# Value rows spaced 72 columns apart in place of 66, in an attention and mixer kernel on one core

## The chip, the core and the metric

The kernel runs on one core of one Trainium2 chip. The metric is the device time of one execution in microseconds; the median of several executions stands for a kernel. The profile is of one such execution.

## The reference

The first half is cosine attention over 8 batches of 12 heads, 448 positions and 64 columns a head. The second half is a low-rank token mixer followed by a two-layer network (768 to 3072 to 768 columns), with residuals.

```python
q_n = q / (norm(q) + 1e-6);  k_n = k / (norm(k) + 1e-6)
scores = q_n @ k_n.T / tau
attn = exp(scores - max(scores));  attn = attn / (sum(attn) + 1e-9)
x = (attn @ v) as [batch, position, 768]
h = x.T @ U @ V                      # rank 32, over positions
u = x + h.T
out = u + relu(u @ w_ch1) @ w_ch2
```

## The kernel before

**Planning.** The kernel does not issue its instructions as it describes them. It adds operations to a planner (`Plan`), each with an engine, an assumed duration, its dependencies and its buffers. The planner simulates the five engines and the order of starts in that simulation becomes the program. TensorE takes its operations from ten streams of fixed priority, and the products below are in one of them (`pe_av`), so that they are put between the long products of the two-layer network (`pe_mlp`). No duration in the plan depends on how the value buffer is laid out.

**Scores and exponents.** For each batch and each pair of heads, `scores` (L677) multiplies keys by queries into PSUM, and ScalarE writes the exponents as bf16 into an `attn` tile (L695, L690), keys on the partitions. There are four key blocks `j`: of 112 keys each in batches 0 and 1, of 128, 128, 128 and 64 in the others, where two neighbouring pairs share one tile for the short block.

**Values.** Two tiles `v_nat` (`v_t`, L327) take turns over the batches. One holds, on each partition, 12 heads by 4 key blocks of rows of D + 2 = 66 bf16 columns: 64 values and two ones. The 65th column makes the product with the exponents also give their sum. The rows are filled by casting DMAs from GpSimd's queue (L516 in batches 0 and 1, L519 and L524 in the others), the ones and the zero halves by memsets on VectorE (`set_v` L1011; `set_v_tiles` L1015, L1017, L1018).

**The product** (`values`, L717 to L721) is a stationary 128-query block of `attn` against one row of 65 columns of `v_nat`. Each head has four query blocks `t`, each a region of 65 columns in one PSUM bank, and each region is summed over the four key blocks:

```python
out=av.tile[:, t, 0:D + 1],
lhsT=(attn if j < SC - 1 else even).tile[0:kp, j, hh, 128 * t:128 * (t + 1)],
rhs=v_t[b % 2][0:kp, h, j, 0:D + 1], start=start, stop=(j == SC - 1),
```

They come in two orders. For all heads but two, `t` is the outer loop and `j` the inner one (L740, L741): four products in a row sum into one region, each from another row of `v_nat`. For the last pair of heads of batch 0 (`ends`, L724 to L731) it is the other way round: for each `j` and head, the four query blocks follow each other, so that four products in a row read the same row of `v_nat` and sum into four different regions. There are 8 x 12 x 16 = 1536 products.

VectorE then takes the reciprocal of the 65th column (L746) and scales the 64 others into `X_sb` (L748). The mixer follows (L801, then L772 and L777 in batch 0, L851 and L865 in the others), then the two-layer network (L928, L951 or L953, L964, L975) and the output DMAs.

Of the kernel before, what the change touches and what calls it, by code (L numbers as in the profile page):

```python
# [12 lines left out]
BF = mybir.dt.bfloat16  # L13
# [256 lines left out]
def kernel(  # L270
# [14 lines left out]
    B, H, S, D = q.shape  # L285
# [7 lines left out]
    SC = 4  # L293
# [18 lines left out]
    def fixed(n, shape, dt, name):  # L312

        tiles = [const.tile(shape, dt, name=f"{name}{i}") for i in range(n)]
        return tiles
# [8 lines left out]
    ld_t = fixed(3, [SCH, 2, G, SC * D], BF, "qk_nat")  # L324
    xn_t = fixed(3, [SCH, 2 * SC, 128], BF, "xn")
    attn_t = fixed(3, [128, SC, 2, 512], BF, "attn")
    v_t = fixed(2, [128, H, SC, D + 2], BF, "v_nat")  # L327

    r_ld, r_xn, r_attn = fixed_ring(ld_t), fixed_ring(xn_t), fixed_ring(attn_t)
    r_sq = ring(2, [SCH, G // 2, SC * D], BF, "sq")  # L330
# [855 lines left out]
```

## Time and profile before

| | |
|---|---|
| median of 9 executions | 585.07 us (584.55 to 586.47) |
| the profiled execution's own time | 585.07 us |
| its span, first to last instruction | 583.3 us |
| mean granted TensorE clock | 0.999 |
| TensorE busy | 573.7 us (98%) |
| VectorE, ScalarE, GpSimd busy | 293.2, 285.0, 93.0 us |
| the 1536 value products (L718): first to last start | 19.1 to 470.7 us |

The profiled execution's time is the median, and 1.8 us of it lie outside the span. A matmul's recorded duration includes its way through the array: consecutive products overlap, so 193 ns is the recorded duration of a value product, while the next one starts some 30 ns after it. What a product costs its engine is the distance from its start to the next start. In a merged row of the timeline, a run of n products lasts n - 1 such distances and one duration.

### The profile page before, as it was taken

Reading aid. Unit: us, or ns where it says so; the run is one execution under the profiler, and the core shown is the slowest. Engines: PE = TensorE matmul, PEld = TensorE weight load, DVE = VectorE, ACT = ScalarE, POOL = GpSimd, SP = SyncE. Lnnn points to the kernel's source line nnn. Section 1 sums busy time; section 2 is a strip of 40 time slices with the busy share of each in tenths; the row PEclk is TensorE's granted clock in tenths of the full one; section 3 lists DMA queues with packets and bytes.
Section 4 is the critical chain, followed back from the end, with each engine's and each line's share of the span. In section 5 each row is a group of like instructions: output and inputs, shape, how many; then the busy total and the mean of one; then the engine's idle time right before and its main releaser. Section 6 shows DMA issues by size and latency. Waiting matters only on the chain.

```text
span 583.3 us, 11692 instructions
## 1 busy us (share of the span) xinstructions
PE 573.7 (98%) x4850; PEld 329.4 (56%) x4871; DVE 293.2 (50%) x690; ACT 285.0 (49%) x471; POOL 93.0 (16%) x134
## 2 busy tenths in 40 slices
PE   8899999999999999999999999999999999999997
PEld 6565656445655665554466655655456666654565
DVE  8979829999656676557434660343102241100011
ACT  7977754677625671466543645434454334024300
POOL 8234240161050132003300140000000000000000
PEclk9999999999999999999999999999999999999999
DMA  9999992997594479346945572231041100310021
GB/s 157 198 207 190 210 159 63 147 130 109 91 124 107 68 80 144 74 78 77 86 88 97 105 49 68 61 74 33 0 67 30 42 15 8 89 40 1 1 54 56
DMA packets 133429, 50.69 MB, mean 87 GB/s; under 512 B 98304, under 2 KB 133376, under 8 KB 133376
## 3 DMA queue, kind: packets, MB, share of 16 engines
q0 software_dynamic: 72256, 25.73, 39.3%
q1 hardware_dynamic: 61056, 24.19, 19.9%
q8 instruction: 38, 0.62, 0.4%
q14 instruction: 15, 0.12, 0.1%
q10 hardware_dynamic: 64, 0.02, 0.0%
HBM read 52.25 MB, written 11.01 MB: 108 GB/s over the span
## 4 chain that ended last, share of the span: by engine, by line
PE 94%; DVE 3%; ACT 1%; issue 1%; DMA 1%; DVEq 0%
PE bank L964 38%; PE bank L928 37%; PE bank L718 8%; PE bank L677 7%; PE bank L851 2%; DVE xn L618 1%; PE bank L474 1%; DVE ss L550 1%; PE bank L801 1%; ACT attn L690 1%; DMA raw_uv<-in_q_dram 1%; ACT sq L544 0%; DVE qkT L1005 0%; PE bank L772 0%; DVE X_sb L748 0%
## 5 line engine op out<-in xcount | busy, mean ns | idle before, releaser
L964 PE MATMUL bank<-w_sb,relu 128*128 128x384 bf16 (+1 forms) x1368 | 231.6, 323 | 0.3 <-DVE X_sb L748 0.2
L928 PE MATMUL bank<-uT,w_sb 128*128 128x384 bf16 (+1 forms) x1132 | 229.8, 352 | 1.2 <-ACT sq L544 0.2
L695 ACT ACTIVATE attn<-bank 128x896 bf16<-128x896 f32 (+1 forms) x166 | 141.1, 916 | 98.5 <-PE bank L677 98.4
L964 PEld LDWEIGHTS <-relu 128*128 128x128 bf16 x1368 | 128.6, 98 | 90.2 <-issue 12.5
L928 PEld LDWEIGHTS <-w_sb 128*128 128x128 bf16 x1152 | 109.1, 98 | 102.3 <-issue 7.6
L951 ACT ACTIVATE relu<-bank 128x384 bf16<-128x384 f32 (+1 forms) x156 | 84.6, 543 | 131.0 <-PE bank L928 130.0
L975 DVE TENSOR_TENSOR O_sb<-bank,u_nat 128x384 f32<-128x384 f32 (+1 forms) x57 | 31.2, 549 | 183.9 <-PE bank L964 162.3
L550 DVE TENSOR_REDUCE ss<-sq 112x8 f32<-112x512 bf16 x96 | 62.4, 673 | 1.9 <-ACT sq L544 1.4
L718 PEld LDWEIGHTS <-attn 128*128 128x128 bf16 (+1 forms) x1536 | 56.0, 98 | 10.0 <-issue 2.8
L618 DVE TENSOR_TENSOR xn<-qk_nat,inv 112x512 bf16<-112x512 bf16 x93 | 60.4, 680 | 0.1
L718 PE MATMUL bank<-v_nat,attn 128*128 128x65 bf16 (+1 forms) x1536 | 59.2, 193 | 0.1
L677 PE MATMUL bank<-qkT 64*128 64x448 bf16 (+1 forms) x384 | 50.1, 358 | 1.5 <-ACT attn L690 0.8
L746 DVE RECIPROCAL rd<-bank 128x4 f32<-128x4 f32 x96 | 16.9, 178 | 59.4 <-PE bank L718 56.6
L496 POOL DMA_DIRECT2D qk_nat<-in_q_dram x24 | 17.3, 723 | 176.6 <-issue 63.3
L748 DVE TENSOR_TENSOR X_sb<-bank,rd 128x256 bf16<-128x256 f32 x96 | 40.2, 421 | 2.0
L544 ACT ACTIVATE sq<-qk_nat 112x512 bf16<-112x512 bf16 x51 | 31.1, 630 | 8.4 <-DVE ss L550 7.9
L519 POOL DMA_DIRECT2D v_nat<-in_v_dram x36 | 26.6, 746 | 49.3 <-PE bank L718 45.4
L953 DVE TENSOR_SCALAR relu<-bank 128x512 bf16<-128x512 f32 (+1 forms) x36 | 22.6, 628 | 14.6 <-PE bank L928 14.4
L677 PEld LDWEIGHTS <-qkT 64*128 64x128 bf16 (+1 forms) x384 | 13.5, 95 | 28.5 <-issue 24.1
L865 DVE TENSOR_TENSOR u_nat<-bank,X_sb 128x384 bf16<-128x384 f32 (+2 forms) x45 | 21.8, 525 | 12.2 <-PE bank L851 12.0
L496 POOL DMA_DIRECT2D qk_nat<-in_k_dram x24 | 16.9, 703 | 4.1 <-DMA w_sb<-in_moe_w_ch_dram 3.6
L546 DVE TENSOR_TENSOR sq<-qk_nat 112x512 bf16<-112x512 bf16 x43 | 16.9, 414 | 0.2
(59 smaller groups left out, 188.5 us busy)
## 6 DMA issues: line engine op xcount, KB each, us to landing
qk_nat<-in_q_dram POOLq DMA_DIRECT2D x23, 224.0 KB, 4.9
qk_nat<-in_k_dram POOLq DMA_DIRECT2D x23, 224.0 KB, 5.7
w_sb<-in_moe_w_ch_dram POOLq DMA_DIRECT2D x4, 1152.0 KB, 21.6
w_sb<-in_moe_w_ch_dram POOLq DMA_DIRECT2D x8, 576.0 KB, 15.9
out_dram<-O_sb SPq DMA_DIRECT2D x15, 168.0 KB, 2.3
v_nat<-in_v_dram POOLq DMA_DIRECT2D x14, 168.0 KB, 9.7
out_dram<-O_sb SPq DMA_DIRECT2D x16, 144.0 KB, 2.1
out_dram<-O_sb SPq DMA_DIRECT2D x16, 120.0 KB, 2.3
```

Of the source, the lines that this page charges most:

```text
L496: ops = [load(lambda i=i, src=src: nc.gpsimd.dma_start(out=ld.tile[:, i, lo:lo + h1 - h0, :], in_=src[b, h0:h1].rearrange("h (s c) d -> s ...
L544: nc.scalar.activation(out=y, in_=x, func=AF.Square)
L550: lambda i=i, a0=a0, a1=a1, sq=sq: nc.vector.reduce_sum(ss.tile[:, i, a0:a1, :].rearrange("p h c -> p (h c)"), sq.tile[:, 0:a1 - a0, :].re ...
L618: nc.vector.tensor_mul(dst, src, sc)
L677: nc.tensor.matmul(out=out, lhsT=qkT.tile.rearrange("p b s -> p (b s)")[r, n0:n0 + w], rhs=qkT.tile[r, SC:2 * SC, :].rearrange("p c s -> p ...
L695: exps.append(plan.add(Op("ACT", act_t(2 * S, 0.08), lambda sc=sc, c=c, attn=attn: nc.scalar.activation(out=attn.tile[0:SCH if b < WIDE el ...
L718: nc.tensor.matmul(out=av.tile[:, t, 0:D + 1], lhsT=(attn if j < SC - 1 else even).tile[0:kp, j, hh, 128 * t:128 * (t + 1)], rhs=v_t[b % 2 ...
L748: muls.append(plan.add(Op("DVE", dve_t(256), lambda av=av, rd=rd, h=h: nc.vector.tensor_mul(X.tile[:, :, h * D:(h + 1) * D], av.tile[:, :, ...
L928: o = plan.add(Op("PE", pe_t(n), lambda cc=cc: nc.tensor.matmul(out=mm.tile[:, 0:n], lhsT=w1_sb[:, cc, f * 128:(f + 1) * 128], rhs=uT.tile ...
L951: nc.scalar.activation(out=relu.tile[:, f, 0:n], in_=mm.tile[:, 0:n], func=AF.Relu)
L964: nc.tensor.matmul(out=mm.tile[:, 0:c1 - c0], lhsT=relu.tile[:, f, i * 128:(i + 1) * 128], rhs=w2_t[:, f, c0:c1], start=(f == 0), stop=(f ...
L975: nc.vector.tensor_add(out=O.tile[:, 0:w], in0=mm.tile[:, 0:w], in1=us[i].tile[:, c0:c1]),
```

## The change

The rows of both value tiles get 72 columns in place of 66. A row is then 144 bytes long in place of 132. The products, the DMAs and the memsets address the same columns as before (64 values and the ones at columns 64 and 65); the columns 66 to 71 are used by nothing, except that the memset of a whole row (L1018) also sets them.

```diff
-    v_t = fixed(2, [128, H, SC, D + 2], BF, "v_nat")
+    v_t = fixed(2, [128, H, SC, D + 8], BF, "v_nat")
```

A tile starts at a multiple of 64 bytes in both kernels. Before, row (h, j) begins 132 (4 h + j) bytes into it, so the four key blocks begin 0, 4, 8 and 12 bytes past a multiple of 16. After, every row begins at a multiple of 16. Each tile grows from 6336 to 6912 bytes on a partition, and every tile that is allocated behind them moves up by 1152 bytes, which is a multiple of 64. The order of instructions is the same on every engine; only the memset at L1018 has another shape, 64 x 216 words in place of 64 x 198.

## Prediction

> **What bounds the kernel now.** I read the page from the top: busy shares and slices, then the chain that ended last.
>
> ```profile
> PE 573.7 (98%) x4850; PEld 329.4 (56%) x4871; DVE 293.2 (50%) x690; ACT 285.0 (49%) x471; POOL 93.0 (16%) x134
> PE   8899999999999999999999999999999999999997
> PEclk9999999999999999999999999999999999999999
> PE 94%; DVE 3%; ACT 1%; issue 1%; DMA 1%; DVEq 0%
> ```
>
> TensorE is busy throughout at full clock and carries 94% of the chain. So a nanosecond taken from each TensorE product comes off the end, and what another engine or a queue does is hidden unless TensorE comes to wait for it. The lines that the change touches, in the groups of instructions and the waits of TensorE after 40 us:
>
> ```profile
> L718 PE MATMUL bank<-v_nat,attn 128*128 128x65 bf16 (+1 forms) x1536 | 59.2, 193 | 0.1
> PE bank L964 <- DVE X_sb L748: 0.2, 1, 0.2
> PE bank L928 <- ACT sq L544: 0.2, 1, 0.2
> ```
>
> The value products waited 0.1 us in all, and after 40 us TensorE waited 0.4 us for other engines. A gain on these products would be kept almost whole.
>
> **What a value product costs now.** I took the start of each of the 1536 records and the distance to the next start where that is a value product too, and sorted the distances by key block j, that is, by how far the row begins past a multiple of 16 bytes. Outside the last head pair of batch 0, leaving out one distance over 60 ns: j = 0 (0 bytes) 29.3 ns on average over 374 distances; j = 1 (4 bytes) 33.2 over 374; j = 2 (8 bytes) 32.5 over 373; j = 3 (12 bytes) 32.6 over 323. For j = 0 the median is 29 for each of the 12 heads.
>
> That looks like the price of a misaligned row: (3.9 + 3.2 + 3.3) ns x 376 query blocks (94 heads by 4) = 3.9 us. But j = 0 differs from the rest in a second way: it opens its PSUM region, and j = 1 to 3 add to the region that the product just before them wrote. The trace holds places where the two come apart. I read these timeline rows:
>
> ```profile
> 34.71 0.78 PE L718 MATMUL bank<-v_nat,attn 112*128 112x65 bf16 x20
> 35.41 0.24 PE L801 MATMUL bank<-X_sb,U_sb 128*32 128x128 bf16 x4
> ...
> 185.34 1.18 PE L718 MATMUL bank<-v_nat,attn 128*128 128x65 bf16 x32
> ```
>
> The row at 185.34 is two heads in the usual order: (1.18 - 0.19) / 31 = 31.8 ns a product, as 8 distances of 29.3 and 23 of about 32.8 would make it. The row at 34.71 belongs to the last head pair of batch 0, where four products in a row read one row of values and go to four different regions. It has 19 distances; the first two, after a wait, are 38 and 36 ns, and the other 17 come to 507 ns, 29.8 each. Of the 20 products 16 read misaligned rows, and 16 add to a region that holds a sum already. At 33 ns a misaligned read, these would take some 33 each; their distances are 30, 29, 32, 29, 30, 29, 32, 29, 30, 29, 33, 29, 29, 30, 29. So neither a misaligned row nor adding as such costs the 3 to 4 ns; adding to the region that was written just before does, or else changing rows does.
>
> The second place:
>
> ```profile
> 58.29 0.35 PE L718 MATMUL bank<-v_nat,attn 112*128 112x65 bf16 x6
> 58.49 0.36 PE L474 MATMUL bank<-ident,xn 112*128 112x112 bf16 x4
> 58.68 0.48 PE L718 MATMUL bank<-v_nat,attn 112*128 112x65 bf16 x10
> ```
>
> Four transposes cut a region's sum in two. The row at 58.68 begins with j = 2, 8 bytes past a multiple of 16, and a row not read just before. Its distance is 29 ns; the next product, j = 3, takes 35, and then j = 0 29 again, j = 1 32. The same cut in batch 1, head 5 lets a j = 1 product start fresh: 29, then 35. A misaligned product on a region that was not written just before costs what an aligned one does. I hold the order of sums to be the cause, and the change does not touch that order.
>
> **The change part by part.** *1128 misaligned products outside the last pair of batch 0* (94 heads x 12): become aligned. Bounds from the rows above: 0 by the two natural tests, -3.9 us by the distances sorted by j. I take 0: the tests change the order and keep the misalignment, the sorting changes both. A loss is excluded by j = 0, whose rows are aligned already and are the quick ones, in heads where they lie at 0 and at 16 past a multiple of 32. *24 in the last pair*: they stand up to 0.8 ns above 29; 0.0 us.
>
> [...]
>
> *Memsets*: four at L1018 grow from 198 to 216 words. One takes 223 ns; 223 x 18/198 = 20 ns at most, 80 ns for all, on VectorE at 38 and 99 us, where the chain runs through TensorE. I take 0; if that cover were gone, +0.08 us.
>
> *Value DMAs*: 43008 packets of 128 bytes, to rows 144 bytes apart in place of 132. Their records last 31 or 32 ns in four of five, in no quarter shorter, though a quarter of the rows begins at a multiple of 16 already. So I expect no change. From batch 1 on the packets end at least 7 us before their first product (50.7 against 58.3 us; 87.4 against 121.7 in batch 2). In batch 0 they run from 10.6 to 18.5 us, and the first product starts at 19.1: 0.6 us of cover, behind which a gain would be hidden too.
>
> *Moved tiles*: all tiles behind the value tiles start 1152 bytes higher, at the same place within 64 bytes. No row shows a price; the nearest are the two 192-column runs of L964 at the end, whose moving rows begin 768 bytes (a multiple of 256) and 1152 bytes (not one) into w2's rows: 82 or 83 ns a product in both. I take 0, and 0.5 us either way, about the middle spread of the nine executions.
>
> Sum: 585.07 + 0 = 585.1 us (the profiled execution's time is the median). About 0.2%, 1.2 us, is what a measurement of this kernel can tell from no change.
>
> **The rivals.** *Alignment is the cause after all* (faster). For it: the clean sorting by offset. It must explain the last pair by the repeated row being free (misaligned rows cost only when they change; the six changes to one there stand at 30, 30, 30, 29, 34 and 34 ns, the first 34 after a wait), and the cut sums by the next row having been fetched during the longer transpose. Both together are possible. [...] Price: 3.9 us, less up to 0.4 us in batch 0 (10 heads x 12 x 3.5 ns), where TensorE waits for ScalarE anyway: 581.2 to 581.6; with the last pair and the spread, 581.0 at the least. A part of it would be between, near 583.
>
> *The value DMA of batch 0 becomes late* (slower). Place: 10.6 to 18.5 us, before the first value product. A packet would have to slow by more than 0.6 / 7.9 = 8% to be felt. If each took 44 ns in place of 32 (some packets do now), 7.9 us become 10.9, and the first product comes 2.3 us late: 587.4. Against it: no dependence on the offset in the packets' records, and those rows at multiples of 16 are written now without notice.
>
> *The change does not do what it says*: excluded; the tiles' starts and the row length in the built program put every row at a multiple of 16.
>
> **How the numbers follow.** No change in the products: 0.69, with its own range 584.5 to 585.7. Alignment the cause, whole or in part: 0.19, of which 0.15 whole. The DMA late: 0.05. Some price of the moved tiles over 0.2%: 0.04 slower, 0.03 faster. That makes 0.22 faster, 0.69 within 0.2%, 0.09 slower. The likeliest case alone holds too little for 8 in 10, so the range reaches down over the alignment case to 581.0, and up to 586.2, the edge of no measurable change; beyond it lie 0.09, and a little below it.
>
> **What would show it.** If I am right, the distances by j stay at 29, 33, 32.5 and 32.6 ns, a two-head run like the one at 185.34 stays at 1.18 us, and the group L718 at 59.2 us. If alignment is the cause, all four stand at 29, the two-head run lasts 31 x 29.3 + 193 = 1.10 us, and the group falls by nearly 4 us. If the DMA is late, the first L718 row starts after 19.2 us and its wait names v_nat. A change of over 1.2 us with the distances unchanged would prove the prediction wrong in a way that I have no step for.

## The result and the profile after

The changed kernel takes 582.74 us (median of 10; 582.49 to 583.79) against 585.07 us (median of 30; 584.40 to 586.47): a ratio of 0.9963, with a 95% interval of 0.9955 to 0.9971. That is 2.3 us faster: outside the likeliest case, and inside the stated range only because that reaches down over a rival. The same lines of the page as before:

```profile
PE 572.0 (98%) x4850; PEld 327.7 (56%) x4871; DVE 292.5 (50%) x690; ACT 284.9 (49%) x471; POOL 93.0 (16%) x134
PEclk9999999999999999999999999999999999999999
PE 94%; DVE 3%; ACT 1%; issue 1%; DMA 1%; DVEq 0%
L718 PE MATMUL bank<-v_nat,attn 128*128 128x65 bf16 (+1 forms) x1536 | 57.1, 193 | 0.1
```

Nothing but TensorE's own work has moved: the chain and the clock are as before, the value products still wait 0.1 us in all, and their busy time fell from 59.2 to 57.1 us. The timeline of TensorE shows it in a run of two heads, and shows no change in the last head pair of batch 0 (the row at 34.10, once 34.71):

```profile
34.10 0.78 PE L718 MATMUL bank<-v_nat,attn 112*128 112x65 bf16 x20
...
184.20 1.14 PE L718 MATMUL bank<-v_nat,attn 128*128 128x65 bf16 x32
```

Two heads last 1.14 us, (1.14 - 0.19) / 31 = 30.6 ns a product, where they lasted 1.18 us. That is neither of the two rows foreseen (1.18 for no effect, 1.10 for aligned rows at 29.3 ns throughout). Sorted by key block as before, over all batches: 30.2, 30.9, 30.6 and 30.2 ns for j = 0 to 3, mean 30.5 where it was 31.9. So j = 1, 2 and 3 became quicker and j = 0 slower. The steady 29, 33, 32, 33 is gone; now most distances are 29 or 30, and about every fifth is 35 (0.215 of those in batches 2 to 7), at all four j, most often at j = 1.

From the first value product to the last matmul of the program the two profiled executions differ by 560.53 - 558.68 = 1.85 us, of which 1.78 came in batches 1 to 7. That is the gain of the products. The first value product itself started 0.53 us earlier, at 18.59 in place of 19.11 us. I don't count that: in the other profiles below it starts between 18.5 and 19.1 us with rows 66 apart and between 18.4 and 19.6 us with rows 72 apart. In the last set of runs below, with both kernels on one chip, the medians differ by 584.95 - 582.84 = 2.1 us.

### The profile page after: what moved, and what is told of

Read it like the earlier page. It is cut to its first block, busy times and chain, and to the rows that moved or that the text cites. A ratio compares the mean times of both kernels' runs of the same rounds, so it can differ in the third digit from the quotient of the medians.

```text
span 580.9 us, 11692 instructions
## 1 busy us (share of the span) xinstructions
PE 572.0 (98%) x4850; PEld 327.7 (56%) x4871; DVE 292.5 (50%) x690; ACT 284.9 (49%) x471; POOL 93.0 (16%) x134
## 4 chain that ended last, share of the span: by engine, by line
PE 94%; DVE 3%; ACT 1%; issue 1%; DMA 1%; DVEq 0%
PE bank L964 38%; PE bank L928 37%; PE bank L718 8%; PE bank L677 7%; PE bank L851 2%; DVE xn L618 1%; PE bank L474 1%; DVE ss L550 1%; PE bank L801 1%; ACT attn L690 1%; DMA raw_uv<-in_q_dram 1%; DVE qkT L1005 0%; ACT sq L544 0%; PE bank L772 0%; DVE X_sb L748 0%
## 5 line engine op out<-in xcount | busy, mean ns | idle before, releaser
L928 PE MATMUL bank<-uT,w_sb 128*128 128x384 bf16 (+1 forms) x1132 | 229.9, 352 | 1.2 <-ACT sq L544 0.2
L928 PEld LDWEIGHTS <-w_sb 128*128 128x128 bf16 x1152 | 109.1, 98 | 102.3 <-issue 7.6
L718 PEld LDWEIGHTS <-attn 128*128 128x128 bf16 (+1 forms) x1536 | 54.1, 97 | 9.9 <-issue 2.8
L718 PE MATMUL bank<-v_nat,attn 128*128 128x65 bf16 (+1 forms) x1536 | 57.1, 193 | 0.1
L677 PEld LDWEIGHTS <-qkT 64*128 64x128 bf16 (+1 forms) x384 | 13.6, 95 | 28.3 <-issue 23.5
```

Of the source, the lines that this page charges most:

```text
L677: nc.tensor.matmul(out=out, lhsT=qkT.tile.rearrange("p b s -> p (b s)")[r, n0:n0 + w], rhs=qkT.tile[r, SC:2 * SC, :].rearrange("p c s -> p ...
L718: nc.tensor.matmul(out=av.tile[:, t, 0:D + 1], lhsT=(attn if j < SC - 1 else even).tile[0:kp, j, hh, 128 * t:128 * (t + 1)], rhs=v_t[b % 2 ...
L928: o = plan.add(Op("PE", pe_t(n), lambda cc=cc: nc.tensor.matmul(out=mm.tile[:, 0:n], lhsT=w1_sb[:, cc, f * 128:(f + 1) * 128], rhs=uT.tile ...
```

## The experiments

All tables and means here are distances from one value product to the next, as in the prediction, of batches 2 to 7, where every product has 128 rows. Before, they are 29.1, 33.1, 32.5 and 32.6 for j = 0 to 3 (mean 31.8); after, 30.0, 31.0, 30.5 and 30.1 (mean 30.4).

The theories: **A**, a row that does not begin at a multiple of 16 bytes costs 3 to 4 ns; **A2**, it does so only where the row changes; **B**, the prediction's: adding to the region just written costs it; **C**, the spacing or the moved tiles matter. **O** and **S** came up on the way.

### Every row off the multiple of 16, in the new spacing

```diff
-    v_t = fixed(2, [128, H, SC, D + 2], BF, "v_nat")
+    v_t = [x[:, :, :, 2:D + 4] for x in fixed(2, [128, H, SC, D + 8], BF, "v_nat")]
```

> Rows 72 columns apart as in the changed kernel, but the data begin 2 columns (4 bytes) into each row, so that every product reads from 4 bytes past a multiple of 16. Theory A (a row that begins off a multiple of 16 bytes costs about 33 ns, one that begins on it about 30.4): all four key blocks at 32.5 to 33 ns, j = 0 too; 1536 x 2.4 ns = 3.7 us slower than the changed kernel, about 1.5 us slower than before: 586.4 us. Theory C (the 144-byte spacing or the moved tiles matter, not where a row begins): distances and time as in the changed kernel, 582.7 us. Theory B (only the order of sums matters, and something else gave the gain): the time cannot be told, but the distances are as in one of the two kernels, with j = 0 the quickest.

582.34 us, ratio to before 0.9960 (0.9947 to 0.9972): as quick as the changed kernel, with every row misaligned. The distances are 29.2, 32.5, 29.2 and 29.1 (mean 30.03). Two heads, 1.18 us before, last

```profile
183.95 1.12 PE L718 MATMUL bank<-v_nat,attn 128*128 128x65 bf16 x32
```

Theory A falls: three of four key blocks stand at 29 ns on misaligned rows. A2 falls with it, as each product here changes its row. Rows begin on a multiple of 16 bytes in the changed kernel, but the gain is not from that. C stands so far. (The 32.5 ns of j = 1, in all its 288 distances, come back in the last section.)

### The order of the sum turned

```diff
-                for j in range(SC):
+                for j in (1, 2, 3, 0):
...
```

The marks of the first and the last product of a region move with the order.

> Rows 66 columns apart as before; only the order of the four key blocks in a region's sum is turned: 1, 2, 3, 0 in place of 0, 1, 2, 3 (the last head pair of batch 0 apart). The product that opens the region is now j = 1, at 4 bytes past a multiple of 16, and j = 0, on the multiple, adds last. Theory A: j = 0 keeps 29.3 ns although it adds to the region just written; j = 1 has 33 although it opens the region. Theory B (adding to the region just written costs the 3 to 4 ns): j = 1 has 29, j = 2, 3, 0 have 33.

One run, 585.15 us. The distances are 29.2, 31.9, 33.0 and 32.6 for j = 0 to 3, and two heads last as long as before:

```profile
185.23 1.17 PE L718 MATMUL bank<-v_nat,attn 128*128 128x65 bf16 x32
```

Theory B falls as well: j = 0 adds last and takes 29.2 ns. What told most is j = 1, which now opens each region. In the first query block of a head, where it follows the j = 0 row of another head or another product, it takes 29 or 30 ns in 72 of 72 cases; in the other three, where it follows the j = 0 row of its own head, 32 to 35 ns in 216 of 216. Same row, same offset, same role in the sum: only what was read just before differs.

### Four query blocks on one row, in both spacings

```diff
-            for t in () if ends else range(4):
-                for j in range(SC):
+            for j in () if ends else range(SC):
+                for t in range(4):
...
```

> Rows 66 columns apart as before, with the order of the last head pair of batch 0 given to all heads: four products in a row read the same row and add to four regions. Theory A, paid at each read: j = 1, 2, 3 stay at 32.5 to 33 ns, mean 31.9, time 585.1 us. Theory A2 (misalignment is paid only where the row changes, once in four): mean about 30.1 ns, 1504 x 1.8 ns = 2.7 us faster than before, 582.4 us. Theory B: all at 29.3 to 30 ns, 582 us or less.

583.34 us, ratio 0.9972 (0.9962 to 0.9982). With rows 66 apart, the first product on j = 1, 2 and 3 takes 33.6 to 34.3 ns (all batches), the three repeats 29.1 to 30.0. So the price is paid at the step from a row to the next one in memory. (On j = 0 it is the second product that has 34.2 ns, which that does not explain.) The mean is 30.5 ns.

The same edit on the changed kernel:

> The changed kernel (rows 72 columns apart) with four products in a row on the same row of values. Theory A: nothing to gain beyond the alignment, mean 30.4 ns with the same sprinkling of 35 ns distances, 582.7 us. Theory A2 (a change of row is what costs, at a lower price where the row is aligned): one change in four, the 35 ns distances become rarer, mean 29.5 ns, 1.3 us faster: 581.4 us.

582.85 us, ratio 0.9970 (0.9959 to 0.9981). With rows 72 apart the order makes no difference: mean 30.4, with 35 ns in 0.218 of the distances (0.215 in the changed kernel). A2's gain of 1.3 us is not there.

What fits all four: with 66 columns, row j ends 2 bytes before row j + 1 begins. **Theory S** says that a product pays where its row begins in the same 16 bytes in which the row read just before it ended. Its rival **O** says that a change of offset pays. In the 4-byte shift no row shares: row 0 ends at byte 133 and row 1 begins at byte 148.

### The same spacing as before, another order of rows

```diff
-                for j in range(SC):
+                for j in (0, 2, 1, 3):
...
```

> The kernel before, rows 66 columns apart, with the four key blocks of a region taken in the order 0, 2, 1, 3. Theory S (new, after the shifted rows turned out quick: a product pays 3 to 4 ns where its row begins in the 16 bytes in which the row read just before it ended, as each row does at 2 bytes' distance from the one before): no product follows the row before its own any more, all four j near 29 ns with some spread, mean 30.1 to 30.5, time 582.3 to 582.9 us with no other spacing at all. Theory A (where a row begins, by itself) and theory O (a change of offset between two products): j = 2, 1, 3 keep 32.5 to 33 ns, 585 us.

29.2, 29.1, 31.9 and 30.5 ns for j = 0 to 3, mean 30.17 where it was 31.8: with offsets that change at each step and no new spacing, the mean falls as far as in the changed kernel, as S has it and A and O have not. Product by product S did not foretell it all. j = 2 follows row 0, shares nothing with it, and still stands at 32 ns or more in 210 of 288 distances; j = 3 does so in 83 of 250. As with j = 1 of the 4-byte shift, 32 ns on one product does not prove sharing. It is the mean over the four that tells: 30.0 to 30.4 without sharing, 31.8 with it at three of four. Nor can C's moved tiles be the cause: no tile has moved here. A run of two heads in its timeline:

```profile
182.96 1.13 PE L718 MATMUL bank<-v_nat,attn 128*128 128x65 bf16 x32
```

The whole kernel gained less than expected: 583.66 us, ratio 0.9972 (0.9960 to 0.9985). In five of its seven runs the mean clock is 0.997 or lower; in the eleven runs of the kernel before beside it, three are. In the profiled one the loss is at the start. The first row has as columns the stretch, its length, the busy time of TensorE, its weight loads, VectorE, ScalarE and GpSimd, the granted clock, the DMA share and GB/s; the two others have TensorE alone:

```profile
0.00:40.00 40.00, 36.05 (x478) 25.37 (x479) 32.85 (x94) 32.86 (x61) 19.35 (x29) 0.96 1.32 185
...
16.30:19.70 3.40, 2.37 (x22) 1.00 1.58 197
19.79:23.20 3.41, 3.41 (x42) 0.50 1.16 210
```

0.96 over 40 us is 1.6 us of clock, where the first 40 us before had 1.00. Value products from 19.8 to 20.4 and from 22.2 to 23.0 us stand 54 to 57 ns apart there. The granted clock is 0.50 for 3.41 us; in the 3.40 us before that it was 1.00, and TensorE was busy for 2.37 of them. The new order of rows is not needed for it: the profile of the next run, in the usual order, has the same loss. What brings it on stays open.

### How wide the shared unit is

```diff
-    v_t = fixed(2, [128, H, SC, D + 2], BF, "v_nat")
+    v_t = fixed(2, [128, H, SC, D + 4], BF, "v_nat")
```

> Rows 68 columns (136 bytes) apart, usual order. Theory S with units of 16 bytes: row 0 ends at byte 129 and row 1 begins at byte 136, in the same 16; row 1 ends at 265, row 2 begins at 272, in the next; row 2 ends at 401, row 3 begins at 408, in the same. So j = 1 and 3 have 33 ns, j = 0 and 2 29 to 30. With units of 8 bytes, or if a distance of 2 bytes is what matters, none shares: all near 30. With units of 32 bytes 1 and 3 share as well, but then the changed kernel should have shown it too.

29.2, 33.2, 29.2 and 32.6 ns, mean 31.0: j = 1 and 3 pay, j = 0 and 2 don't. The one run took 584.01 us, which says little, as its clock fell at the start too:

```profile
0.00:40.00 40.00, 36.35 (x482) 25.27 (x483) 33.87 (x96) 33.12 (x61) 19.62 (x30) 0.96 1.30 186
```

Ends and beginnings 6 bytes apart still share a price, so it is not the 2 bytes. Not 8 bytes, as bytes 129 and 136 lie in different eights. Not 32, as in the changed kernel bytes 129 and 144 lie in the same 32 and j = 1 is rid of the steady 33. Theory A would give the same four numbers here; the next run parts them.

### One column less, in both spacings

```diff
-            nc.tensor.matmul(out=av.tile[:, t, 0:D + 1],
+            nc.tensor.matmul(out=av.tile[:, t, 0:D],
...
-                             rhs=v_t[b % 2][0:kp, h, j, 0:D + 1], start=start, stop=(j == SC - 1),
+                             rhs=v_t[b % 2][0:kp, h, j, 0:D], start=start, stop=(j == SC - 1),
...
-                out=rd.tile, in_=av.tile[:, :, D:D + 1]), deps=[o], acq=[rd], prio=1))
+                out=rd.tile, in_=av.tile[:, :, D - 1:D]), deps=[o], acq=[rd], prio=1))
```

> Rows 66 columns apart as before, but each product takes 64 columns in place of 65 (the sum of the exponents is left out, and the last value column is divided by in its place). Theory S: row 0 now ends at byte 127 and row 1 begins at byte 132, not in the same 16, so j = 1 falls to about 29 ns; j = 2 and 3 still share (259 and 264, 391 and 396) and stay at 32 to 33. Theory A or O: j = 1, 2 and 3 all stay at 32 to 33.

One run, 583.03 us. 28.3, 28.5, 33.0 and 31.7 ns. Nothing about where rows begin has changed, but row 0 now ends at byte 127 and no longer shares with row 1, and j = 1 alone drops from 33.1 to 28.5 ns. Theories A and O can't do that; S foretold it. (This kernel and the next leave out the sum of the exponents: they measure products and are no versions to use.) In its timeline two heads last

```profile
182.18 1.13 PE L718 MATMUL bank<-v_nat,attn 128*128 128x64 bf16 x32
```

> Rows 72 columns apart, each product takes 64 columns (the sum left out in the same way). What is left of the changed kernel is a distance of 35 ns once in about five products, mean 30.4. If the 65th column, alone in its ninth 16 bytes, makes it: none of 35 left, mean 28.8 to 29.2. If it is a limit on the rate of products whatever they read: mean stays at 30 or over, 35 once in five.

One run, 581.00 us, and no distance of 35 ns is left: 29.1 to 29.2 for all four j.

```profile
183.60 1.10 PE L718 MATMUL bank<-v_nat,attn 128*128 128x64 bf16 x32
```

So the 35 ns distances of the changed kernel belong to its 65th column: with it a product takes 30.4 ns, without it 29.1. One column of a long product is (162.7 / 384) = 0.4 ns, so the length alone does not explain it. The 65th column is also what makes a row touch a ninth 16 bytes, alone there; this run doesn't part the two, and the next section shows what being alone adds.

### Other offsets, and long products

```diff
-    v_t = fixed(2, [128, H, SC, D + 2], BF, "v_nat")
+    v_t = [x[:, :, :, 4:D + 6] for x in fixed(2, [128, H, SC, D + 8], BF, "v_nat")]
```

> Rows 72 columns apart, data beginning 4 columns (8 bytes) in: every row begins 8 bytes past a multiple of 16, no row shares its 16 bytes with another, and its first and last 16 bytes give 4 and 5 columns, in place of 8 and 1 in the changed kernel. Theory S: none pays 3 to 4 ns at each change. If the lone 65th column makes the 35 ns distances: none of 35, mean 30.0 as in the 4-byte shift or a little under, 582.3 us. If nine pieces of 16 bytes for 65 columns are the limit wherever they are cut: mean 30.0 too, as 9 x 8 columns at 2.4 columns a ns; the changed kernel's 30.4 is then its own. Theory A: 32.5 to 33 ns throughout, 586 us.

582.79 us, ratio 0.9965 (0.9952 to 0.9979). Mean 30.03; no distance of 35, one in five of 33 or 34. The 2.4 columns a ns of the expectation follow from L928's rows, where 128 columns more take 216.1 - 162.7 = 53.4 ns. With five columns in the ninth 16 bytes in place of one, the surplus over 29.1 falls from 1.3 to 0.9 ns and does not go. The changed kernel and the 4-byte shift again, on the same chip:

> The changed kernel again, beside the two shifted ones on one chip: 582.7 us, mean distance 30.4 ns with 35 ns once in five.

> The 4-byte shift again, beside the changed kernel on one chip: mean distance 30.05 ns, 33 ns at j = 1 alone. If the 0.35 ns a product below the changed kernel reach the end: 0.5 us quicker than that, 582.3 us.

582.84 us (0.9962; 0.9950 to 0.9975) and 582.85 us (0.9957; 0.9944 to 0.9971), means 30.39 and 30.03. The 0.36 ns a product, 0.5 us over all, can't be seen in the times. No version that computes the whole result was measurably better than the changed kernel.

On the changed kernel, the second weight's rows:

```diff
-    w2_t = const.tile([128, NC, C], BF, name="w2_sb")
+    w2_t = const.tile([128, NC, C + 2], BF, name="w2_sb")
...
-            out=w2_t[:, i * w:(i + 1) * w, :],
+            out=w2_t[:, i * w:(i + 1) * w, 0:C],
```

> The changed kernel, with the rows of the second weight 770 columns (1540 bytes) apart in place of 768, so that three of four of L964's 384-column products read a row that begins 4, 8 or 12 bytes past a multiple of 16; no row begins where the one read before it ended. Theory S: no cost, 162 to 163 ns a product as before, 582.7 us. Theory A, now for long products: 3 to 4 ns for three of four, 1416 x 0.75 x 3.5 ns = 3.7 us slower than the changed kernel, 586.4 us.

One run, 583.29 us. Of the 384-column products one in four now stands at 165 ns and the one before it at 161 or 162; the mean of all goes from 162.8 to 162.9 ns. Misaligned rows cost these long products 0.1 ns, next to nothing; whether a shared 16 bytes would cost them was not tried, as no row here begins where the one before it ended. A single run can't tell the 0.15 us that 0.1 ns makes.

## Why the prediction was wrong

**The reading of the profile held.** TensorE bounds the kernel, and what the products lose comes off the end: over all batches the distances fell by 31.87 - 30.48 = 1.39 ns, for 1504 products 2.1 us; 1.85 us of it was seen between the first value product and the end. Batch 0 kept next to none of its share (0.07 us), as the rival's price foresaw.

**The step that failed** is "I hold the order of sums to be the cause", and with it the term of the 1128 misaligned products, taken as 0. It measured 1.85 us, or 2.1 by the mean distances. Both natural tests took away more than I saw. In the last pair of batch 0 a product follows the same row or a row of another head; behind the transposes it follows another tile. In both, the row read just before does not end where the new row begins, and so neither pays the steady price, whatever it adds to. I had written that "adding to the region that was written just before does, or else changing rows does", and then dropped the second half. The turned order shows the first half wrong, the cut to 64 columns shows what the second half must be: not changing rows, but going on to a row in the same 16 bytes. A test that keeps the suspect (here the offset) and drops its price proves only that the suspect needs a partner.

**The flat price**, 33.2, 32.5 and 32.6 ns at 4, 8 and 12 bytes, spoke against theory A, which the 4-byte shift refuted. It is just what sharing gives: all three began in the 16 bytes of their forerunner, and j = 0 did not. So the rival that I gave 0.19, alignment, was wrong about the cause too; that the range, stretched for it, took in the result, and that the result lies near its "part of it" at 583, is luck. A multiple of 16 bytes is merely one way to keep rows apart; rows 4 bytes off it gained as much.

**The rival's size was off too**: 3.9 us was for rows at 29.3 ns. Those of before ran at 29.3 only between slower ones; alone among their like they come to 30.4. That leaves 1.39 of the 2.6 ns. The runs show 30.4 ns where one column is alone in the ninth 16 bytes, 30.03 where the first and last 16 bytes give 6 and 3 or 4 and 5 columns, 29.1 where there is no ninth. The larger price was that of sharing: 1.9 to 2.4 ns net for a product that shares, against a surplus of 0.9 to 1.3 ns over 29.1 without sharing.

**The small terms** fell as set: the memsets at L1018 take 238 ns in place of 223 and nothing waits for them, and the value DMAs have no effect on the products. The 0.6 us of cover in batch 0 is real and thin: where the first products came early, they waited for v_nat (0.5 us in the 4-byte shift's profile), in rows 66 and 72 apart alike:

```profile
18.46 0.25 PE L718 MATMUL bank<-v_nat,attn 112*128 112x65 bf16 x3
19.16 0.55 PE L718 MATMUL bank<-v_nat,attn 112*128 112x65 bf16 x13 [0.45 <-DMA v_nat<-in_v_dram]
```

## What to carry to other kernels

Where short products (of 65 columns here) read consecutive rows, see that no row begins in the 16 bytes in which the one before it ended: pad the rows, or visit them in another order. A product that paid took some 3.5 ns more here (32.5 to 33.2 against 29.1 to 29.2), a tenth of a 65-column product. Freeing all of them gained less here, 1.4 ns on the mean, as the quick products did not stay at 29.2 ns once the ones between them that paid were gone. Long products were not tried with shared rows. When the trace offers a natural test, list everything that it changes before giving the price to one cause, above all what the engine read just before.

## What the runs showed of the hardware

- A 65-column product that begins in the 16 bytes in which the moving row just before it ended takes 32.5 to 33.2 ns from start to start (33.6 to 34.3 with four query blocks on one row); one that does not takes 29.1 to 29.2 when products that pay lie between. The unit is 16 bytes by the runs with rows 66, 68 and 72 apart.
- Without any sharing, 65 columns do not hold 29.2 ns: the mean is 30.03 to 30.4 ns over four ways of laying out and ordering the rows, and 29.14 for 64 columns. An estimate from the rows: L928's products of 512 and 384 columns stand 216.1 and 162.7 ns apart, 0.417 ns a column; nine pieces of eight columns would take 30.0 ns. The surplus over 29.1 comes as single distances, of 32 to 34 ns (offsets 4 and 8) or 35 ns (offset 0), once in four to five products; at the 4-byte offset they settle on j = 1, in the order 0, 2, 1, 3 on j = 2 and 3. Why so is open, and so what a product pays cannot be read from one distance: against layouts without sharing, a shared product costs 1.9 to 2.4 ns net, worked out from (31.8 - 30.4) and (31.8 - 30.03) over three products in four.
- The start of the first value product varies by 1.2 us over the profiles (18.4 to 19.6 us), with no tie to the layout: the 4-byte shift alone has 18.46 and 19.60 us.
